# Top-k attention with a mixture of experts on one core: the scores of two heads copied out of PSUM together

## The chip, the cores and the metric

One core of one Trainium2 chip runs the program. The metric is device time in microseconds (us). The kernel before took 651.46 us (median of 3 runs, 651.18 to 654.83). The profile comes from one more execution of 652.79 us.

## The reference

Three parts follow each other. All the work of this case is in the first, the attention:

```python
B, H, S, D = 2, 8, 576, 64            # q, k, v
scores = q @ k.T / sqrt(D)            # per batch and head: 576 x 576
kth = 32nd largest of each row
attn = softmax(where(scores >= kth, scores, -1e9))
x = attn @ v                          # then 1152 tokens x 512
```

Then each token goes to one of 8 experts (`argmax` of 8 gate logits, at most 288 tokens for each), two matmuls with a ReLU between; then a dense layer 512 to 2048 to 512 with `h * clip(h + 3, 0, 6) / 6`. All is float32.

## The kernel before, in words

The attention is cut into 72 units: 9 tiles of 128 tokens by 8 heads. A unit u is one head of one tile, so its scores are 128 rows of 576 columns. Tile 4 holds 64 tokens of each batch; its units 32 to 39 take a query of all 128 rows (two heads, the other half zeros), and their last product is done in two halves.

Nothing is scheduled by the tool: the order is written out. A loop over steps i = 0 to 72 (L568) runs a string of letters, `STEP = "RGXCYTZEMAQLB"` (L36), and each letter issues one block for a unit that lies a fixed number of steps back or ahead (L557). Each engine takes its own instructions in that order, in a queue. The letters that matter here, with the engine, and the unit in step i:

| letter | what | engine, lines | unit |
|---|---|---|---|
| C | `cut_excess` | ScalarE (ACT), L337 | i - 1 |
| Y | `fetch`: scores from PSUM to SBUF | ACT, L313 | i + 2 |
| Z | `shift` | ACT, L396 | i - 3 |
| E | `expo`, out of PSUM | ACT, L421 | i - 4 |
| M | `below`, the mask of what is under the 32nd value | ACT, L400 | i - 3 |
| T | `ptr`: five transposes of Z's result, each with M's mask added by a matmul | TensorE (PE), L414, L415 | i - 4 |
| A | `attv`: five products with v | PE, L432 | i - 5 |
| Q | `qk`: scores of units i + 3 and i + 4, in odd steps alone | PE, L304 | i + 3, i + 4 |
| R, L | the search for the 32 largest | VectorE (DVE), L328 to L364 | |
| X, B | two subtractions of 128x576 | GpSimd (POOL), L334, L340 | |

On ACT a step is C, Y, Z, E, M; on PE it is T, A and in odd steps Q. T of a step reads what Z and M of the step before wrote, E reads what T of the same step wrote, A what E of the step before wrote. Q writes two PSUM tiles of two banks each (`ps_s`, L194); the copies Y of the next even step and of the odd step after it read them. Pairs of heads lie on rows 0 to 63 and 64 to 127, so the two products of a pair run beside each other on the array; in units 32 to 39 they take all rows and run one after the other.

Four times (steps 11, 15, 19, 23, and in each of steps 1 to 4) a block `mix` (L443) stands ahead of a step: ten PE records and two small ACT copies. In steps 43, 49, 55, 61 a scaled copy `xg` (L515, ACT) and an indirect DMA follow the step.

The experts begin after the attention, and then the dense layer; both are long runs of matmuls.

Of the kernel before, what the change touches and what calls it, by code (L numbers as in the profile page):

```python
# [8 lines left out]
F32 = mybir.dt.float32  # L9
F32R = mybir.dt.float32r  # L10
BF = mybir.dt.bfloat16
I32 = mybir.dt.int32
U32 = mybir.dt.uint32
AF = mybir.ActivationFunctionType
OP = mybir.AluOpType
AX = mybir.AxisListType
PS = bass.MemoryType.PSUM

P = 128
B, H, S, D = 2, 8, 576, 64  # L20
# [18 lines left out]
RING = 8  # L39
# [19 lines left out]
def topk_attention_moe_ffn_kernel(ctx, tc, qT, kT, vx, vT, wg, w1, w2, w_in, w_out, out, cap):  # L59
    nc = tc.nc  # L60
    W = 192
# [24 lines left out]
    rows = wp.tile([1, 2, E], F32, name="rows")  # L86
# [104 lines left out]
    with ExitStack() as actx:  # L191
        big = actx.enter_context(tc.tile_pool(name="big", bufs=1))
        wk = actx.enter_context(tc.tile_pool(name="wk", bufs=2))
        ps_s = actx.enter_context(tc.tile_pool(name="ps_s", bufs=2, space=PS))  # L194
        ps_t = actx.enter_context(tc.tile_pool(name="ps_t", bufs=1, space=PS))
        ps_o = actx.enter_context(tc.tile_pool(name="ps_o", bufs=2, space=PS))

# [10 lines left out]
        kt = big.tile([P, B, HP, S], F32, name="kt")  # L208
# [51 lines left out]
        for i in range(2):  # L260
            u = big.tile([P, 5 * P], F32, name=f"ub{i}")
# [18 lines left out]
        st, st2, tops, ends = {}, {}, {}, {}  # L280
        av, cuts = {}, {}
# [6 lines left out]
        def split(u):  # L288
            t, h = divmod(u, H)
            if t == 4:  # L290
                hp, b = h // 4 * 2 + h % 4 // 2, h % 2
                return [(b, 2 * hp + r, slice(b * 64, b * 64 + 64), slice(r * 64, r * 64 + 64)) for r in range(2)]
            return [(t // 5, h, slice(0, P), slice(0, P))]

        def qk(*us):
            todo = []
            for u in us:
                b, h = split(u)[0][:2]
                t, r0 = u // H, h % 2 * D
                rows, q = (slice(0, P), qts[b * 5 + 4]) if t == 4 else (slice(r0, r0 + D), qts[t])  # L300
                todo.append((u, ps_s.tile([P, 2, 512], F32, name="ps"), q[rows, h // 2], kt[rows, b, h // 2]))
            for c in range(2):
                for _, ps, q, k in todo:
                    nc.tensor.matmul(ps[:, c, :288], q, k[:, c * 288:(c + 1) * 288], start=True, stop=True)  # L304
            for u, ps, _, _ in todo:
                st[u] = ps

        def fetch(u):
            ps = st[u]
            slab = wk.tile([P, S * 3 // 2], F32, name="s", bufs=RING)  # L310
            cuts[u] = slab[:, S:].bitcast(BF)
            st[u] = slab[:, :S]
            nc.scalar.activation(st[u].rearrange("p (a b) -> p a b", a=2), ps[:, :, :288], AF.Copy)  # L313

        def interleave(*chains):
            chains = [list(c) for c in chains]
            n = max([1] + [len(c) for c in chains])
            for i in range(n):
                for ops in chains:
                    for f in ops[i * len(ops) // n:(i + 1) * len(ops) // n]:  # L320
                        f()
# [12 lines left out]
            nc.gpsimd.tensor_tensor(s2, s, lists[t % 2][:, h, KEEP * NCK:, None].to_broadcast([P, NCK, CW]), op=OP.subtract)  # L334

        def cut_excess(u):
            nc.scalar.activation(cuts[u], st2[u], AF.Relu, scale=PUSH)  # L337

        def drop_excess(u):
# [13 lines left out]
        def merge(u):  # L353
            t, h = divmod(u, H)
            l = lists[t % 2][:, h, NE - KT:KEEP * NCK]
            m = wk.tile([P, 2, KT], F32, name="m2")
            l2 = wk.tile([P, KEEP * NCK - NE + KT], F32, name="l2")
            end = ends.pop(u)
            for i in range(2):
                yield lambda i=i: nc.vector.max(m[:, i], l2 if i else l)  # L360
                yield lambda i=i: nc.vector.match_replace(out=l2, in_to_replace=m[:, i], in_values=l2 if i else l,
                                                          imm_value=LOW)
            yield lambda: nc.vector.max(end[:, NE:], l2)
            yield lambda: nc.vector.max(tops[t][:, h, KT:], end)  # L364
# [37 lines left out]
        def part(u):  # L402
            t, h = divmod(u, H)
            nc.vector.tensor_scalar(ubufs[u % 2][:, :S], st[u], -1.0, tops[t][:, h, 0:1], op0=OP.mult, op1=OP.add)

        def mask(u):
            t, h = divmod(u, H)
            nc.vector.tensor_scalar(lbufs[u % 2][:, :S], st.pop(u), tops[t][:, h, 2 * KT - 1:], None, op0=OP.is_lt)

        def ptr(u):  # L410
            pt = ps_t.tile([P, 8, P], F32, name="pt")
            for c in range(5):
                cs = slice(c * P, (c + 1) * P)
                nc.tensor.matmul(pt[:, c], ubufs[u % 2][:, cs], ident, is_transpose=True, start=True, stop=False)  # L414
                nc.tensor.matmul(pt[:, c], lbufs[u % 2][:, cs], drop, start=False, stop=True)  # L415
            st[u] = pt

        def expo(u):
            pt = st[u]
            pts = wk.tile([P, 5, P], F32, name="pts")  # L420
            nc.scalar.activation(pts, pt[:, :5], AF.Exp, scale=-SCALE)  # L421
            st[u] = pts

        def attv(u):
            t, g = u // H, u % H // 4
            pts = st.pop(u)
            if (t, g) not in av:
                av[t, g] = temp([P, 4, VC], "av")
            for b, h, rows, cols in split(u):
                for c in range(5):  # L430
                    at = (2 * c + h % 2) * VS
                    nc.tensor.matmul(av[t, g][rows, h % 4], pts[:, c, cols], vt[b, h // 2][:, at:at + VC],  # L432
                                     start=c == 0, stop=c == 4)

        def norm(t, h0, h1, rows=slice(0, P)):
            o = av.pop((t, h0 // 4))[rows, h0 % 4:h0 % 4 + h1 - h0]
            rs = wk.tile([P, 4, 1], F32, name="rs")[rows, :h1 - h0]
            yield lambda: nc.vector.tensor_scalar(rs, o[:, :, VS - 1:VS], 1e-9, None, op0=OP.add)
            yield lambda: nc.vector.reciprocal(rs, rs)
            yield lambda: nc.vector.tensor_tensor(x_tok[rows, t, h0:h1], o[:, :, :VS - 1],  # L440
                                                  rs.to_broadcast(list(o.shape[:2]) + [VS - 1]), op=OP.mult)
# [83 lines left out]
        def keep_warm(n, out):  # L525
            for _ in range(n):
                nc.tensor.matmul(out, dummy[:, :P], dummy, start=True, stop=True)
# [32 lines left out]
        keep_warm(KW, wm)  # L560
        load_q(2)
        qk(0, 1)
        fetch(0)
        fetch(1)
        qk(2, 3)
        for i in range(LEAD):
            interleave(round1(i))
        for i in range(NU + 1):  # L568
# [17 lines left out]
            for a, b, at, gap in ROUTES:  # L586
# [3 lines left out]
                n, r = divmod(i - at - 2, gap)  # L590
# [9 lines left out]
        u = NU - 1  # L600
        round2(u)
        interleave(merge(u - 1), merge(u), norm(NT - 1, 0, 4), routes[NU - 1][3])
        spare = ps_s.tile([P, 2, 512], F32, name="ps")[:, 0]
        warm = lambda n: keep_warm(n, spare)
        send = lambda t: scatter(t) if t >= sent else None
        for f, *args in ((ptr, u - 2), (expo, u - 2), (attv, u - 3), (send, 4), (send, 5), (attv, u - 2), (warm, 5),
# [10 lines left out]
        def redo(u):  # L617
            t, h = divmod(u, H)
            qk(u)
            fetch(u)  # L620
            s = st[u]
            tops[t] = wk.tile([P, H, 2 * KT], F32, name="tops")
            top = wk.tile([P, TOPK], F32, name="ends", bufs=4)
            m = top
            cur = s
            for i in range(4):
                nc.vector.max(m[:, 8 * i:8 * i + 8], cur)
                if i < 3:
                    nxt = wk.tile([P, S], F32, name="s2", bufs=3)
                    nc.vector.match_replace(out=nxt, in_to_replace=m[:, 8 * i:8 * i + 8], in_values=cur, imm_value=LOW)  # L630
                    cur = nxt
            nc.vector.tensor_copy(tops[t][:, h, 0:1], m[:, 0:1])
            nc.vector.tensor_copy(tops[t][:, h, 2 * KT - 1:], m[:, TOPK - 1:])
            part(u)
            mask(u)
            ptr(u)
            expo(u)
            last = (t, h // 4) in av
            attv(u)
            if last:  # L640
                return
            for n, (_, h, rows, _) in enumerate(split(u)):
                if n:
                    av[t, h // 4] = o
                o = av[t, h // 4]
                interleave(norm(t, h, h + 1, rows))
# [3 lines left out]
        with tc.If(at(0) > 0):  # L650
# [11 lines left out]
            for t in range(NT - 2):  # L662
# [2 lines left out]
            scale(NT - 2, xg_last[NT - 2])  # L665
            pick(NT - 2)
        room[0] = ps_o, "o"
        spare = ps_s.tile([P, 2, 512], F32, name="ps")[:, 0]

        t = NT - 1  # L670
        banks = [pool.tile([P, 2, 512], F32, name=name)[:, 0, :2 * W].rearrange("p (a w) -> p a w", a=2)
                 for pool, name in ((ps_s, "ps"), (ps_t, "pt"))]
        warm(WARM[0])
        interleave(norm(t, 4, H))
        x_pick(banks, xg_last[NT - 2], NT - 2, True)
# [11 lines left out]
    with ExitStack() as mctx:  # L687
# [59 lines left out]
        with ExitStack() as ectx:  # L747
            eb = ectx.enter_context(tc.tile_pool(name="eb", bufs=2))
            ps = ectx.enter_context(tc.tile_pool(name="ps", bufs=8, space=PS))
# [154 lines left out]
        ps = mctx.enter_context(tc.tile_pool(name="ps2", bufs=2, space=PS))  # L904
# [111 lines left out]
```

## Time and profile before

| | |
|---|---|
| median of the runs | 651.46 us |
| profiled execution | 652.79 us, span of the trace 651.0 us |
| PE busy | 614.4 us, 94% |
| ACT busy | 369.7 us, 57% |
| DVE busy | 370.6 us, 57% |
| POOL busy | 285.5 us, 44% |
| attention steps | from about 5 to 250 us of the span |
| copies of scores (L313) | 72, 48.4 us in all |

The shares are means over stages with different limits. In the attention ACT, PE and DVE are all at nine tenths or more; in the experts and the dense layer PE alone is. A busy time is the union of the spans of an engine's instructions. Two neighbours on ACT overlap by about a tenth of a us in the trace, so what an instruction takes of its engine is read from start to start, and when its result is there from its start and its duration.

### The profile page before, as it was taken

What the parts mean: (1) busy time and instruction counts of PE and PEld (TensorE: products, weight loads), DVE (VectorE), ACT (ScalarE), POOL (GpSimd) and SP (SyncE); (2) the same over time, 40 slices, a digit from 0 to 9 for tenths busy, and PEclk for the clock granted to TensorE, in tenths of its full rate; (3) what the DMA queues carried; (4) which work ended last, traced back from release to release, by engine and by line L of the source; (5) the groups of instructions that cost most, each with busy time, mean ns of one, the idle gap of its engine ahead of it and who ended that gap; (6) DMA issues with size and microseconds to landing.
All of it is one profiled execution on the core that took longest, in us unless ns stands there. A gap on an engine that the chain in (4) does not pass through costs nothing.

```text
span 651.0 us, 11922 instructions
## 1 busy us (share of the span) xinstructions
PE 614.4 (94%) x4085; PEld 549.7 (84%) x4085; DVE 370.6 (57%) x1838; ACT 369.7 (57%) x687; POOL 285.5 (44%) x337
## 2 busy tenths in 40 slices
PE   7899999999989987799999999999999999999996
PEld 4687878888767775699999999998988999999995
DVE  3899999999899994211233333334756655222221
ACT  3899999989999983111233343344555544242222
POOL 5787878869789962000234222222432342030001
PEclk9899999999999998899999999999999999999999
DMA  8529700100000002297789977712331320010001
GB/s 284 183 69 367 239 2 17 34 3 18 18 17 3 16 2 80 103 332 289 188 258 284 306 285 263 254 65 65 98 98 65 97 65 1 0 66 33 1 1 48
DMA packets 37054, 75.13 MB, mean 115 GB/s; under 512 B 4016, under 2 KB 12464, under 8 KB 36976
## 3 DMA queue, kind: packets, MB, share of 16 engines
q1 hardware_dynamic: 35248, 69.47, 32.4%
q0 software_dynamic: 1728, 4.72, 1.9%
q8 instruction: 36, 0.59, 0.4%
q14 instruction: 42, 0.34, 0.2%
HBM read 64.75 MB, written 9.44 MB: 114 GB/s over the span
## 4 chain that ended last, share of the span: by engine, by line
PE 42%; issue 14%; POOL 2%; ACT 0%; POOLq 0%; DVE 0%; ACTq 0%; DVEq 0%
PE hps L806 13%; PE yps L806 13%; PE h L915 8%; PE acc L929 7%; POOL out_dram L938 1%; PE xp L769 1%; POOL cm__12092 L723 0%; POOLq L1012 0%; POOL spacer L937 0%; ACT cg__11220 L715 0%; POOL fw L730 0%; ACT fw L729 0%; ACT gh L922 0%; DVE cg__11220 L717 0%; DVE x2l L826 0%
## 5 line engine op out<-in xcount | busy, mean ns | idle before, releaser
L328 DVE MAX8 lists<-s 128x8 f32<-128x72 f32 x576 | 127.5, 228 | 17.3 <-ACT s L313 17.1
L340 POOL TENSOR_TENSOR s<-s 128x576 f32<-128x576 f32 x72 | 92.5, 1285 | 34.2 <-ACT s L337 33.8
L915 PE MATMUL h<-x2h,fw 128*128 128x384 f32 x384 | 98.5, 337 | 0.9 <-DVE x2l L826 0.9
L432 PE MATMUL av<-vt,pts 128*128 128x96 f32 (+1 forms) x800 | 99.3, 273 | 0.0
L432 PEld LDWEIGHTS av<-vt,pts 128*128 128x128 f32 (+1 forms) x800 | 91.0, 182 | 2.1 <-issue 0.9
L806 PE MATMUL yps<-hT,wslot 128*128 128x192 f32 x512 | 90.8, 326 | 0.0
L806 PE MATMUL hps<-xe,wslot 128*128 128x192 f32 x512 | 86.4, 330 | 3.5 <-DVEq L844 2.9
L929 PE MATMUL acc<-fw,gh 128*128 128x512 f32 x288 | 89.4, 391 | 0.0
L806 PEld LDWEIGHTS hps<-xe,wslot 128*128 128x128 f32 x512 | 85.1, 193 | 4.1 <-ACT xg L858 3.4
L334 POOL TENSOR_TENSOR s<-s,lists 128x576 f32<-128x576 f32 x72 | 82.9, 1152 | 4.8 <-DVE lists L328 3.6
L806 PEld LDWEIGHTS yps<-hT,wslot 128*128 128x128 f32 x512 | 82.1, 190 | 1.2
L414 PE MATMUL pt<-ident,ub 128*128 128x128 f32 x360 | 76.2, 289 | 6.7 <-ACT pts L421 6.1
L415 PE MATMUL pt<-drop,lb 128*128 128x128 bf16 x360 | 66.2, 221 | 9.4 <-ACT lb L400 9.4
L915 PEld LDWEIGHTS h<-x2h,fw 128*128 128x128 f32 x384 | 70.2, 188 | 5.0 <-DVE x2l L826 1.2
L414 PEld LDWEIGHTS pt<-ident,ub 128*128 128x128 f32 x360 | 51.1, 142 | 25.5 <-ACT pts L421 9.9
L915 PE MATMUL h<-x2l,fw 128*128 128x384 f32 x192 | 64.8, 337 | 0.0
L929 PEld LDWEIGHTS acc<-fw,gh 128*128 128x128 f32 x288 | 53.4, 187 | 8.3
L918 ACT ACTIVATE g<-h,three 128x384 f32<-128x384 f32 x48 | 27.9, 581 | 56.2 <-PE h L915 56.2
L919 DVE SCALAR_TENSOR_TENSOR g<-g,h 128x384 f32<-128x384 f32 x48 | 26.5, 552 | 54.7 <-ACT g L918 54.2
L400 ACT ACTIVATE lb<-s,tops 128x576 bf16<-128x576 f32 x71 | 57.6, 811 | 0.0
L922 ACT CAST gh<-g 128x384 fp32r<-128x384 f32 x48 | 24.6, 513 | 56.8 <-PE acc L929 52.1
L396 ACT ACTIVATE ub<-s,tops 128x576 f32<-128x576 f32 x70 | 56.6, 809 | 0.0
(411 smaller groups left out, 1018.7 us busy)
## 6 DMA issues: line engine op xcount, KB each, us to landing
wslot<-in_w_dram SPq DMA_DIRECT2D x15, 2048.0 KB, 9.7
raw<-in_w_in_dram SPq DMA_DIRECT2D x16, 512.0 KB, 3.7
raw<-in_w_out_dram SPq DMA_DIRECT2D x16, 512.0 KB, 3.6
xs<-x_tok SPq DMA_DIRECT2D x8, 576.0 KB, 13.0
vt<-in_vx_dram SPq DMA_DIRECT2D x8, 365.0 KB, 4.6
kt<-in_kT_dram SPq DMA_DIRECT2D x8, 288.0 KB, 4.3
vts<-in_vT_dram SPq DMA_DIRECT2D x8, 288.0 KB, 4.1
qt<-in_qT_dram SPq DMA_DIRECT2D x9, 256.0 KB, 4.6
```

The source lines that it names most:

```text
L328: yield lambda c=c: nc.vector.max(lists[t % 2][:, h, c::NCK], st[u][:, c * CW:(c + 1) * CW])
L334: nc.gpsimd.tensor_tensor(s2, s, lists[t % 2][:, h, KEEP * NCK:, None].to_broadcast([P, NCK, CW]), op=OP.subtract)
L340: nc.gpsimd.tensor_tensor(st2[u], st[u], cuts.pop(u), op=OP.subtract)
L396: nc.scalar.activation(ubufs[u % 2][:, :S], st[u], AF.Identity, bias=tops[t][:, h, 0:1], scale=-1.0)
L400: nc.scalar.activation(lbufs[u % 2][:, :S], st.pop(u), AF.Relu, bias=tops[t][:, h, 2 * KT - 1:], scale=-1.0)
L414: nc.tensor.matmul(pt[:, c], ubufs[u % 2][:, cs], ident, is_transpose=True, start=True, stop=False)
L415: nc.tensor.matmul(pt[:, c], lbufs[u % 2][:, cs], drop, start=False, stop=True)
L432: nc.tensor.matmul(av[t, g][rows, h % 4], pts[:, c, cols], vt[b, h // 2][:, at:at + VC], start=c == 0, stop=c == 4)
L806: nc.tensor.matmul(out, wb[:, k], m[:, k, :self.w], start=first and k == 0, stop=last and k == HP - 1)
L915: nc.tensor.matmul(h2, fw[f][:, 0, a, k * P:(k + 1) * P], (x2h, x2l)[b][:, k, c * CH:(c + 1) * CH], start=n == 0, stop=n == len(ops) - 1)
L918: nc.scalar.activation(g, h2, AF.Relu, bias=three)
L929: nc.tensor.matmul(acc[j], g[a][:, j * P:(j + 1) * P], fw[f][:, 1, b], start=f == 0 and n == 0, stop=f == NF - 1 and n == 2)
```

## The change

The two score tiles of a pair become one PSUM tile of four banks with one buffer. Q writes its two halves with the same matmuls in the same order. `fetch` does nothing for odd units; for an even one, one ACT instruction copies both halves, 1152 columns, into one SBUF tile for two units. There are four such tiles where there were eight single ones. The result of C, which lay behind each unit's scores in the same buffer, gets a small tile of its own (three buffers). At the end of the attention two later users of that PSUM, the target of the idle matmuls (`spare`) and the first of `banks`, are two banks of one tile.

```diff
-        ps_s = actx.enter_context(tc.tile_pool(name="ps_s", bufs=2, space=PS))
+        ps_s = actx.enter_context(tc.tile_pool(name="ps_s", bufs=1, space=PS))
...
         def qk(*us):
             todo = []
+            room_s = ps_s.tile([P, 2, 2, 512], F32, name="ps")
+            st[us[0]] = room_s
             for u in us:
...
-                todo.append((u, ps_s.tile([P, 2, 512], F32, name="ps"), q[rows, h // 2], kt[rows, b, h // 2]))
+                todo.append((u, room_s[:, len(todo)], q[rows, h // 2], kt[rows, b, h // 2]))
...
-        def fetch(u):
+        def fetch(u, n=2):
+            if n == 2 and u % 2:
+                return
             ps = st[u]
-            slab = wk.tile([P, S * 3 // 2], F32, name="s", bufs=RING)
-            cuts[u] = slab[:, S:].bitcast(BF)
-            st[u] = slab[:, :S]
-            nc.scalar.activation(st[u].rearrange("p (a b) -> p a b", a=2), ps[:, :, :288], AF.Copy)
+            slab = wk.tile([P, 2, S], F32, name="s", bufs=RING // 2)
+            for i in range(n):
+                st[u + i] = slab[:, i]
+            nc.scalar.activation(slab[:, :n].rearrange("p u (a b) -> p u a b", a=2), ps[:, :n, :, :288], AF.Copy)
...
         def cut_excess(u):
+            cuts[u] = wk.tile([P, S], BF, name="cut", bufs=3)
             nc.scalar.activation(cuts[u], st2[u], AF.Relu, scale=PUSH)
...
         qk(0, 1)
         fetch(0)
-        fetch(1)
         qk(2, 3)
...
-        spare = ps_s.tile([P, 2, 512], F32, name="ps")[:, 0]
+        ends_ps = ps_s.tile([P, 2, 2, 512], F32, name="ps")
+        spare = ends_ps[:, 1, 0]
```

ACT, two steps from the first tile, an odd and then an even one, before (`s<-s` is C, `s<-ps` is Y, `ub` is Z, `pts` is E, `lb` is M):

```order
L337 ACTIVATE s<-s_571 128x576 [waits Pool_49]
L313 ACTIVATE s<-ps 128x576
L396 ACTIVATE ub_188<-s,tops 128x576 [waits Activation_49]
L421 ACTIVATE pts<-pt 128x640 [waits PE_49,Activation_49]
L400 ACTIVATE lb_190<-s,tops 128x576 [waits DVE_49,Activation_49]
L337 ACTIVATE s<-s_621 128x576 [waits Pool_49]
L313 ACTIVATE s<-ps 128x576 [waits PE_49]
L396 ACTIVATE ub_192<-s,tops 128x576 [waits Activation_49]
L421 ACTIVATE pts<-pt 128x640 [waits PE_49,Activation_49]
L400 ACTIVATE lb_194<-s,tops 128x576 [waits DVE_49,Activation_49]
```

The same two steps now:

```order
L340 ACTIVATE cut<-s_562 128x576 [waits Pool_49]
L399 ACTIVATE ub_188<-s,tops 128x576 [waits Activation_49]
L424 ACTIVATE pts<-pt 128x640 [waits PE_49,Activation_49]
L403 ACTIVATE lb_190<-s,tops 128x576 [waits DVE_49,Activation_49]
L340 ACTIVATE cut<-s_613 128x576 [waits Pool_49]
L315 ACTIVATE s<-ps 128x1152 [waits PE_49,Activation_49]
L399 ACTIVATE ub_192<-s,tops 128x576
L424 ACTIVATE pts<-pt 128x640 [waits PE_49]
L403 ACTIVATE lb_194<-s,tops 128x576 [waits DVE_49]
```

The odd step has lost its copy; the copy of the even step is twice as wide and still stands ahead of Z, E and M of its step, behind a wait for PE.

PE, the end of an odd step and the start of the next, before (`av` is A, `ps` is Q, `pt` is T):

```order
L432 MATMUL av<-vt_118,pts 128x96 x4
L304 MATMUL ps<-kt,qt 128x288
L304 MATMUL ps<-kt,qt 128x288 [waits Activation_49]
L304 MATMUL ps<-kt,qt 128x288 x2
L414 MATMUL pt<-ident,ub_188 128x128 [waits Activation_49]
L415 LDWEIGHTS lb_190 [waits Activation_49]
```

And now:

```order
L435 MATMUL av<-vt_118,pts 128x96 x4
L306 MATMUL ps<-kt,qt 128x288 x4
L417 MATMUL pt<-ident,ub_188 128x128 [waits Activation_49]
L418 LDWEIGHTS lb_190 [waits Activation_49]
```

Q no longer waits inside for the copy of the odd step; its place behind A and ahead of T is as it was. SP's queue is the same in both.

## Rows read from the trace of the kernel before

**Rows 1.** Busy us of PE, PEld, DVE, ACT, POOL in one stretch; granted clock, DMA.

```profile
90.00:130.00 40.00, 38.23 (x315) 32.86 (x315) 38.35 (x265) 39.52 (x65) 34.28 (x42) 1.00 0.07 21
```

**Rows 2.** ACT in order of time, one pair of steps: start us, duration us, line.

```profile
63.06 0.78 ACT L400 ACTIVATE lb<-s,tops 128x576 bf16<-128x576 f32 x1
63.72 0.69 ACT L337 ACTIVATE s<-s 128x576 bf16<-128x576 f32 x1
64.30 0.65 ACT L313 ACTIVATE s<-ps 128x576 f32<-128x576 f32 x1
...
66.75 0.69 ACT L337 ACTIVATE s<-s 128x576 bf16<-128x576 f32 x1
67.32 0.65 ACT L313 ACTIVATE s<-ps 128x576 f32<-128x576 f32 x1
67.85 0.79 ACT L396 ACTIVATE ub<-s,tops 128x576 f32<-128x576 f32 x1
68.52 0.71 ACT L421 ACTIVATE pts<-pt 128x640 f32<-128x640 f32 x1
69.10 0.79 ACT L400 ACTIVATE lb<-s,tops 128x576 bf16<-128x576 f32 x1
```

**Rows 3.** PE in order of time, the same pair; idle before and its releaser in brackets.

```profile
63.89 0.23 PE L415 MATMUL pt<-drop,lb 128*128 128x128 bf16 x1 [0.34 <-ACT lb L400]
...
64.64 1.31 PE L432 MATMUL av<-vt,pts 128*128 128x96 f32 x10
65.88 1.24 PE L304 MATMUL ps<-kt,qt 64*128 64x288 f32 x8
67.05 0.33 PE L414 MATMUL pt<-ident,ub 128*128 128x128 f32 x1
```

**Rows 4.** Waits of ACT from 30 to 234 us: us in total, times, longest.

```profile
ACT s L313 <- PE ps L304: 1.0, 2, 0.6
```

**Rows 5.** ACT, two of its lines: duration ns min/median/max, forms.

```profile
L313 ACT ACTIVATE s<-ps x72: 633/652/827, 6.3 to 231.2; 128x576 f32<-128x576 f32 x72
L816 ACT ACTIVATE hT<-hps x64: 314/331/332, 271.0 to 433.2; 128x192 f32<-128x192 f32 x64
```

**Rows 6.** PE in order of time, units of tile 4 in A.

```profile
130.27 1.24 PE L304 MATMUL ps<-kt,qt 64*128 64x288 f32 x8
...
134.41 0.22 PE L415 MATMUL pt<-drop,lb 128*128 128x128 bf16 x1
```

**Rows 7.** ACT, the same stretch.

```profile
131.54 0.65 ACT L313 ACTIVATE s<-ps 128x576 f32<-128x576 f32 x1 [0.37 <-PE ps L304]
...
133.34 0.77 ACT L400 ACTIVATE lb<-s,tops 128x576 bf16<-128x576 f32 x1
```

**Rows 8.** PE, units of tile 4 in Q.

```profile
110.32 2.13 PE L304 MATMUL ps<-kt,qt 128*128 128x288 f32 x8
```

**Rows 9.** ACT, M of the even steps around that Q.

```profile
107.60 0.76 ACT L400 ACTIVATE lb<-s,tops 128x576 bf16<-128x576 f32 x1
...
114.00 0.77 ACT L400 ACTIVATE lb<-s,tops 128x576 bf16<-128x576 f32 x1
```

**Rows 10.** PE at a step with `mix`.

```profile
69.10 1.37 PE L447 MATMUL mix<-wg_sb,vts 128*128 128x96 f32 x10
```

**Rows 11.** PE, Q in the first steps.

```profile
8.74 1.24 PE L304 MATMUL ps<-kt,qt 64*128 64x288 f32 x8 [2.51 <-DMA kt<-in_kT_dram]
...
12.84 1.23 PE L304 MATMUL ps<-kt,qt 64*128 64x288 f32 x6 [0.27 <-ACT s L313]
...
18.30 1.23 PE L304 MATMUL ps<-kt,qt 64*128 64x288 f32 x6 [0.62 <-ACT s L313]
```

**Rows 12.** Busy us by stretch as in group 1, in the clock's dip.

```profile
24.00:26.00 2.00, 1.70 (x11) 1.45 (x12) 1.84 (x14) 2.00 (x5) 1.36 (x2) 0.60 0.60 230
26.00:28.00 2.00, 2.00 (x12) 1.88 (x11) 2.00 (x16) 1.85 (x4) 1.36 (x3) 0.55 0.01 3
```

**Rows 13.** The chain that ended last, its first long piece after the attention.

```profile
269.40 11.91 PE hps L806 x62
```

More of the change, by code (lines that the diff above doesn't have):

```diff
@@ L304, in qk @@
                     nc.tensor.matmul(ps[:, c, :288], q, k[:, c * 288:(c + 1) * 288], start=True, stop=True)
-            for u, ps, _, _ in todo:
-                st[u] = ps
-        def fetch(u):
+        def fetch(u, n=2):
+            if n == 2 and u % 2:
+                return
             ps = st[u]
-            slab = wk.tile([P, S * 3 // 2], F32, name="s", bufs=RING)
-            cuts[u] = slab[:, S:].bitcast(BF)
-            st[u] = slab[:, :S]
-            nc.scalar.activation(st[u].rearrange("p (a b) -> p a b", a=2), ps[:, :, :288], AF.Copy)
+            slab = wk.tile([P, 2, S], F32, name="s", bufs=RING // 2)
+            for i in range(n):
+                st[u + i] = slab[:, i]
+            nc.scalar.activation(slab[:, :n].rearrange("p u (a b) -> p u a b", a=2), ps[:, :n, :, :288], AF.Copy)
         def interleave(*chains):
@@ L602, in topk_attention_moe_ffn_kernel @@
         interleave(merge(u - 1), merge(u), norm(NT - 1, 0, 4), routes[NU - 1][3])
-        spare = ps_s.tile([P, 2, 512], F32, name="ps")[:, 0]
+        spare = ps_s.tile([P, 2, 2, 512], F32, name="ps")[:, 0, 0]
         warm = lambda n: keep_warm(n, spare)
@@ L619, in redo @@
             qk(u)
-            fetch(u)
+            fetch(u, 1)
             s = st[u]
@@ L667, in topk_attention_moe_ffn_kernel @@
         room[0] = ps_o, "o"
-        spare = ps_s.tile([P, 2, 512], F32, name="ps")[:, 0]
+        ends_ps = ps_s.tile([P, 2, 2, 512], F32, name="ps")
+        spare = ends_ps[:, 1, 0]
         t = NT - 1
-        banks = [pool.tile([P, 2, 512], F32, name=name)[:, 0, :2 * W].rearrange("p (a w) -> p a w", a=2)
-                 for pool, name in ((ps_s, "ps"), (ps_t, "pt"))]
+        banks = [tile[:, :2 * W].rearrange("p (a w) -> p a w", a=2)
+                 for tile in (ends_ps[:, 0, 0], ps_t.tile([P, 2, 512], F32, name="pt")[:, 0])]
         warm(WARM[0])
```

## The prediction

> **What bounds the kernel now.** I read the busy time by stretch first. In a 40 us stretch of the attention ACT is busy 39.5 us, DVE 38.4, PE 38.2, POOL 34.3 [rows 1]. ACT is the fullest, but three others are near, so a share tells little: what matters is which wait returns to ACT. Then ACT and PE in order of time over one pair of steps. ACT runs without a gap: from M of one even step to M of the next it takes 69.10 - 63.06 = 6.04 us, a start every 0.53 to 0.67 us [rows 2]. PE waits 0.34 us for M's mask, then does the rest of T, then A, then Q [rows 3]. So a loop goes round both engines once a pair: M of the even step, T, A and Q of the odd step, copy Y, Z, E, M of the next even step. It is nearly as long as ACT's own work. M ends at 63.06 + 0.78 = 63.84; PE goes on at 63.89; Q starts at 65.88 and ends at 67.12 [rows 2, 3]; a copy that does wait for Q starts 0.03 us after its end (131.54 against 130.27 + 1.24) [rows 6, 7]. So the copy could have started at 67.15, and started at 67.32 [rows 2]: **the slack of the loop is 0.17 us.** That is why ACT waits for Q only twice, 1.0 us in all, between 30 and 234 us [rows 4]. What the attention loses or gains is passed on whole, since the experts' matmuls begin only after it [rows 13].
>
> **The change, part by part.**
>
> *ACT's own work.* 36 copies go and 36 grow. The copy takes 0.53 us from its start to Z's (67.32 to 67.85) [rows 2]. Per element, from the shortest copy of 576 and the shortest ACT instruction of 192 columns out of PSUM: (633 - 314) / 384 = 0.831 ns [rows 5], so 576 more columns cost 0.48 us. A pair saves 0.53 - 0.48 = 0.05 us, 1.8 us in all, if nothing but ACT counts. The Trainium skill (ScalarE: Activation LUTs, "What ACT_TABLE_LOAD costs") has neighbours overlap by about 93 ns, so each removed instruction would give that much, as an estimate 36 x 93 ns = 3.3 us; its 0.833 ns an element agrees with the trace's 0.831.
>
> *The loop.* All of the wide copy now stands between Q and M: 0.48 us more, where the loop had 0.17. From a row where the copy did wait, copy start to M's end is 133.34 + 0.77 - 131.54 = 2.57 us [rows 7]; the wide copy makes it 3.05. A plain pair is then: M's end to Q's end 67.12 - 63.84 = 3.28, plus 0.03, plus 3.05 = 6.36 us, against 6.04 to 6.05 now: **0.31 us more.** ACT then idles before the wide copy. The bounds of the second half are 0.48 (elements alone) and 0.53 (a whole further copy [rows 2]); I take 0.48, since it is one instruction.
>
> *The pairs*, by the odd step that holds Q; there are 34:
> - 11 plain ones (7, 25, 27, 45, 47, 53, 57, 59, 63, 65, 67): 11 x 0.31 = **3.4 us.**
> - Four with units of tile 4 in Q (29 to 35). The two heads run one after the other; Q takes 2.13 us, and the old copy needed only the first head. Now it waits for both. M ends at 107.60 + 0.76 = 108.36, Q at 110.32 + 2.13 = 112.45, so the next M ends at 112.45 + 0.03 + 3.05 = 115.53: 7.17 us, where M to M was 6.40 [rows 8, 9]. 4 x 0.77 = **3.1 us.**
> - Four with units of tile 4 in A (37 to 43). Here PE runs without a gap, and M's end (134.11) is 0.30 us ahead of the matmul that needs it (134.41) [rows 6, 7], 0.25 us with the 0.05 us that PE takes to start. The first such pair loses 0.48, the others about 0.24 each: **1.2 us.**
> - Eight with `mix` or just ahead of it (9 to 23): `mix` holds PE for 1.37 us between A and T [rows 10], so M may come 0.31 us later before T notices. **0**; the cover is PE's own work, and without it this would be another 2.5 us.
> - Four with the scaled copy for a scatter, or right behind one (49, 51, 55, 61): it fills the place that the odd copy leaves on ACT, so ACT and not Q is last there. **0.**
> - The first three (1 to 5). The first wide copy ends 0.48 us later, but the second Q waits for a transfer until 8.74 us anyway. After it Q waits twice for the copy of the odd step, 0.27 and 0.62 us [rows 11]; that copy is now done a step earlier, so both waits go: **-0.9 us.** Right behind lies a dip of TensorE's clock to 0.60 and 0.55 of full speed from 24 to 28 us [rows 12]; I leave it as it is. If the moved work escapes it, 2 x 0.40 + 2 x 0.45 = 1.7 us more is saved.
>
> *What else moves.* DVE may begin the search in a new pair only when the wide copy is done, 0.48 us later after its start, but has 38.35 of 40 us of work, 5.8 us in a pair of 6.05 [rows 1], so 0.56 us of room in 6.36. POOL has more. C's result in a tile of its own changes no transfer and no order. Q's PSUM is read out some 4 us before the next Q needs it, so one buffer costs PE nothing in the loop. The two PSUM users at the end keep their order on PE. All these: 0.
>
> **Sum**: 3.4 + 3.1 + 1.2 + 0 + 0 - 0.9 = 6.8 us. Against the profiled execution, 652.79, that is 659.6; it lay 1.3 us above the median, 651.46, which becomes **658.3 us.**
>
> **The rivals.**
> - *ACT alone is the bound* (not slower). If the loop had 0.48 us of slack or more, the change would give 0.05 us a pair: 651.5 - 1.8 = 649.7 us. It decides on one number, the time from Q's end to the copy's start in plain pairs. For it: ACT has no gaps [rows 2]. Against it: that time is 0.20 us, of which 0.03 is the wait itself. By the Trainium skill's 93 ns (ScalarE: Activation LUTs, the same section) it would be 648.2. Chance 0.08.
> - *Only the tight places pay.* If plain pairs have some slack that I don't see (a copy that starts reading sooner, a shorter T), what is left is 3.1 + 1.2 - 0.9 = 3.4 us: 654.9 us. For it: ACT hardly ever waits for Q now [rows 4]. Against: the starts fit to 0.05 us all along the pair. Chance 0.12.
> - *A further engine joins the loop.* If DVE, with its later start, holds M back, the pair grows by the rest of the 0.48 us too: 34 x 0.17 = 5.8 us more, 664 us. Or PE's longer gaps (in the four wide pairs over 1 us of 7.17) bring the clock down as at 24 us: each such dip costs 1.7 us, three of them 663 us. For it: DVE is 96% busy [rows 1]. Against: the clock stands at 1.00 through that stretch with PE not quite full, and DVE has the 0.56 us. Chance 0.12.
>
> **How the numbers follow.** The forecast has 0.68. Its own range: down by the clock's dip, 1.7, and some of the places called 0; up by 0.05 us in 19 pairs, 1.0, and 0.3 for the end of the attention: 656.0 to 659.5. The range reaches down to the second rival and up by half of the third: 654 to 662, which leaves out the first and most of the third, 0.2. A measurement of this kernel tells about 1% from no change, 6.5 us or 658.0. The forecast lies on that line: I give 0.38 of its 0.68 to slower by more, as the dip probably stays, 0.30 to within. With the rivals: slower 0.38 + 0.11 = 0.49; within 0.30 + 0.08 + 0.12 = 0.50, less 0.01 for the unforeseen; faster 0.02.
>
> **What would show it.** ACT should wait for Q (`s` of the copy behind `ps`) in nearly every pair between 30 and 234 us, about 0.4 us in a plain pair, where it now does twice. A plain pair should take 6.36 us from M to M, one with units of tile 4 in Q 7.17, one with `mix` what it takes now. The wide copy should last 1.12 us. The wait of 0.62 us in the first steps should be gone. It is wrong if ACT has no gap before the wide copy, if the gap is there and M to M still stays at 6.05, or if DVE or POOL is what M waits for.

## The result, and the profile after

The changed kernel takes 663.67 us in the median (four runs, 660.55 to 665.72). The kernel before stands at 653.14 over four runs, the three behind 651.46 and one more. The ratio is **1.0145, 95% interval 1.0108 to 1.0182: slower by about 9.5 us** (the medians lie 10.5 us apart). The forecast was 6.8 us more, and 658.3 us. The two profiled executions stand at 662.85 and 652.79 us.

The stretch of 40 us again, as in [rows 1]:

```profile
90.00:130.00 40.00, 35.47 (x277) 29.88 (x278) 34.59 (x241) 34.87 (x53) 31.93 (x41) 1.00 0.03 9
```

Every engine is busy for less of it: ACT 34.87 us instead of 39.52, PE 35.47 instead of 38.23. No engine became the bound; all of them wait more. ACT in order of time over one pair shows where (Q in step 9; like the pair of [rows 2] it lies just ahead of `mix`, and it takes what a plain pair takes):

```profile
37.51 0.77 ACT L403 ACTIVATE lb<-s,tops 128x576 bf16<-128x576 f32 x1
38.18 0.68 ACT L340 ACTIVATE cut<-s 128x576 bf16<-128x576 f32 x1
38.75 0.77 ACT L399 ACTIVATE ub<-s,tops 128x576 f32<-128x576 f32 x1
...
40.67 0.68 ACT L340 ACTIVATE cut<-s 128x576 bf16<-128x576 f32 x1
41.68 1.13 ACT L315 ACTIVATE s<-ps 128x1152 f32<-128x1152 f32 x1 [0.33 <-PE ps L306]
42.70 0.77 ACT L399 ACTIVATE ub<-s,tops 128x576 f32<-128x576 f32 x1
43.37 0.69 ACT L424 ACTIVATE pts<-pt 128x640 f32<-128x640 f32 x1
43.95 0.77 ACT L403 ACTIVATE lb<-s,tops 128x576 bf16<-128x576 f32 x1
```

And PE over the same pair:

```profile
38.34 0.23 PE L418 MATMUL pt<-drop,lb 128*128 128x128 bf16 x1 [0.34 <-ACT lb L403]
...
39.09 1.31 PE L435 MATMUL av<-vt,pts 128*128 128x96 f32 x10
40.33 1.24 PE L306 MATMUL ps<-kt,qt 64*128 64x288 f32 x8
```

These answer to [rows 2] and [rows 3]. M to M is 43.95 - 37.51 = 6.44 us, where it was 6.04. The loop is to be seen whole: M's end 38.28, PE goes on at 38.34, Q ends at 40.33 + 1.24 = 41.57. ACT has been waiting since cut ended, and starts the wide copy at 41.68. From M's end to Q's end it is 3.29 us, as before (3.28). What has grown is the copy (1.13 us), and the time from Q's end to its start, 0.11 us.

Waits of ACT, 30 to 234 us, as in [rows 4]:

```profile
ACT s L315 <- PE ps L306: 11.4, 21, 1.1
```

1.0 us in 2 waits have become 11.4 us in 21. They are the plain pairs, those just ahead of `mix` and those with units of tile 4, but for one. The copy's line by itself, with durations in ns (min, median, max), answers to [rows 5]:

```profile
L315 ACT ACTIVATE s<-ps x36: 1113/1131/1133, 7.5 to 237.2; 128x1152 f32<-128x1152 f32 x36
L315 ACTq EVENT_SEMAPHORE  x31: 17/17/17, 28.7 to 237.1; - x31
```

The second row is new: ahead of 31 of the 36 copies ACT's queue runs an instruction that only waits. The Trainium skill (Perfetto Trace Analysis, "Identifying Dependency Chains") says that an instruction with waits on several engines may get such a one ahead of it for the further wait; experiment 5 bears that out.

With units of tile 4 in Q, the rows that answer to [rows 8, 9]:

```profile
105.31 0.77 ACT L403 ACTIVATE lb<-s,tops 128x576 bf16<-128x576 f32 x1
...
107.78 1.13 ACT L315 ACTIVATE s<-ps 128x1152 f32<-128x1152 f32 x1 [1.12 <-PE ps L306]
...
112.54 0.77 ACT L403 ACTIVATE lb<-s,tops 128x576 bf16<-128x576 f32 x1
```

M to M is 7.23 us there, and ACT waits for 1.12 of them.

**The sum by place.** All pairs, from the end of M in one even step to the next, in the two profiles:

| pairs | forecast, us each | measured, us each | forecast, sum | measured, sum |
|---|---|---|---|---|
| 11 plain | 0.31 | 0.38 | 3.4 | 4.2 |
| 4 with units of tile 4 in Q | 0.77 | 0.83 | 3.1 | 3.3 |
| 4 with units of tile 4 in A | 0.48, 0.24 x 3 | 0.56, 0.33, 0.25, 0.42 | 1.2 | 1.6 |
| 4 just ahead of `mix` | 0 | 0.38 | 0 | 1.5 |
| 4 with `mix` | 0 | -0.29 | 0 | -1.1 |
| 4 at the scatters | 0 | -0.06 to -0.02 | 0 | -0.2 |
| from M of step 6 to M of step 68 | | | **7.7** | **9.2** |

A second profile of each kernel (experiments 8 and 12) gives this stretch as 199.15 us before (199.12 in the first) and 208.35 after (208.37). So the 9.2 us are of the kernel, to 0.03 us. What lies ahead of step 6 and between the attention and the experts is not so firm; it comes in the experiments.

### The profile page after: what moved, and what is told of

The parts are those of the page before. It is cut to its first block, busy times and chain, and to the rows that moved or that the text cites. A ratio compares the mean times of both kernels' runs of the same rounds, so it can differ in the third digit from the quotient of the medians.

```text
span 661.0 us, 11850 instructions
## 1 busy us (share of the span) xinstructions
PE 617.2 (93%) x4085; PEld 550.8 (83%) x4085; DVE 369.7 (56%) x1838; ACT 369.5 (56%) x651; POOL 286.1 (43%) x337
## 4 chain that ended last, share of the span: by engine, by line
PE 41%; issue 14%; POOL 2%; ACT 0%; POOLq 0%; DVE 0%; ACTq 0%; DVEq 0%
PE hps L809 13%; PE yps L809 12%; PE h L918 8%; PE acc L932 7%; POOL out_dram L941 1%; PE xp L772 1%; POOL cm__12055 L726 0%; POOLq L1015 0%; POOL spacer L940 0%; ACT cg__11183 L718 0%; POOL fw L733 0%; ACT fw L732 0%; ACT gh L925 0%; DVE cg__11183 L720 0%; DVE x2l L829 0%
## 5 line engine op out<-in xcount | busy, mean ns | idle before, releaser
L343 POOL TENSOR_TENSOR s<-s,cut 128x576 f32<-128x576 f32 x72 | 92.5, 1285 | 39.7 <-ACT cut L340 37.9
L932 PE MATMUL acc<-fw,gl 128*128 128x512 f32 x144 | 56.5, 392 | 0.0
L926 DVE TENSOR_TENSOR gl<-g,gh 128x384 fp32r<-128x384 f32 x48 | 27.4, 571 | 50.4 <-ACT gh L925 50.4
```

The costliest lines, as they stand in the source:

```text
L343: nc.gpsimd.tensor_tensor(st2[u], st[u], cuts.pop(u), op=OP.subtract)
L926: nc.vector.tensor_tensor(gl, g, gh.bitcast(F32), op=OP.subtract)
L932: nc.tensor.matmul(acc[j], g[a][:, j * P:(j + 1) * P], fw[f][:, 1, b], start=f == 0 and n == 0, stop=f == NF - 1 and n == 2)
```

## The experiments

My theory was that of the prediction: a loop through PE and ACT, M, T, A, Q, copy, Z, E, M, which the copy's width makes longer. The rivals were that DVE, which starts its search later, holds M back (the third rival of the prediction), and that the shared PSUM tile, not the width, costs the time. "M to M" is meant as above.

**1. q_ahead.** Q is put ahead of T and A, so that it no longer stands between M and the wide copy.

```
-STEP = "RGXCYTZEMAQLB"
+STEP = "RGXCYQTZEMALB"
```

> The changed kernel with one letter of the step's order moved: Q (the scores of the next pair, on PE) stands ahead of T and A of its odd step, not behind them. The wide copy stays as it is. My theory (the wide copy lies in a loop M, T, A, Q, copy, Z, E, M that goes round PE and ACT once a pair): Q then ends long before the copy's turn on ACT, the loop is cut, ACT is the bound again with the 0.05 us it saved a pair. M to M of a plain pair 6.0 to 6.1 us (changed kernel 6.44, before 6.06), with units of tile 4 in Q 6.1 to 6.3 (7.23); ACT hardly waits for Q; time 0.993 to 1.001 of before. Rival 1 (one instruction over four PSUM banks or one PSUM buffer costs by itself): M to M stays near 6.44, ratio near 1.0145. Rival 2 (DVE or POOL has joined the loop because a pair's scores come at once): M to M 6.2 to 6.4 and DVE or POOL named in front of M or C.

Measured: 651.06 us against 655.72 for the kernel before beside it, ratio **0.9927, interval 0.9899 to 0.9955**. ACT in a pair:

```profile
43.66 0.67 ACT L340 ACTIVATE cut<-s 128x576 bf16<-128x576 f32 x1
44.23 1.12 ACT L315 ACTIVATE s<-ps 128x1152 f32<-128x1152 f32 x1
45.24 0.77 ACT L399 ACTIVATE ub<-s,tops 128x576 f32<-128x576 f32 x1
```

No gap stands ahead of the wide copy any more. A plain pair takes 6.00 us instead of 6.44. With units of tile 4 in Q it takes 6.40, which is less than 7.23 but not the 6.1 to 6.3 expected. The first steps, by stretches as in [rows 12]:

```profile
22.00:24.00 2.00, 1.66 (x18) 1.59 (x18) 2.00 (x15) 2.00 (x4) 1.70 (x2) 1.00 0.92 355
24.00:26.00 2.00, 1.68 (x18) 1.43 (x17) 2.00 (x18) 2.00 (x4) 1.94 (x3) 1.00 0.10 38
26.00:28.00 2.00, 2.00 (x17) 1.44 (x15) 2.00 (x15) 2.00 (x4) 1.73 (x2) 1.00 0.00 0
```

The clock stays at 1.00 where it stood at 0.60 and 0.55. M of step 6 ends at 28.31 us, 3.5 earlier than in the first profile of before; from there to step 68 it is 198.25 us against 199.12. So the change with Q moved is faster than both kernels, and most of that gain lies in the first steps. The width costs nothing once it stands off the loop.

**2. copy_last.** Q stays where it is, and the copy goes to the end of ACT's step instead, behind M.

```
-STEP = "RGXCYTZEMAQLB"
+STEP = "RGXCTZEMYAQLB"
```

> The changed kernel with the copy Y moved behind M in its even step on ACT (order C, Z, E, M, Y); Q stays behind T and A. My theory: Z, E and M no longer stand behind the wait for Q, the loop is cut at another place, M to M of a plain pair 6.0 to 6.1 us; DVE gets the scores some 2 us later in the pair and may wait more, up to 6.2. Time 0.993 to 1.004 of before. Rival 1 (the wide instruction costs by itself): near 6.44 and 1.0145 as in the changed kernel. Rival 2 (DVE is what is short): slower than the changed kernel, above 1.015, with DVE's idle time in front of the search grown by over 0.4 us a pair.

Measured: 666.44 us, ratio 1.0154, interval 1.0113 to 1.0195. A miss for my theory. Plain pairs mostly alternate between 7.12 and 6.35 us. Waits from 30 to 245 us:

```profile
POOL s L336 <- DVE lists L347: 36.3, 34, 2.3
...
DVE lists L330 <- ACT s L315: 23.0, 30, 1.1
...
ACT lb L403 <- DVE tops L367: 11.0, 15, 1.1
```

Now ACT's M waits for DVE's tops, 15 times, since the search began late. So the rival with DVE is real, one move further on: the copy has a place that is too late for PE's loop and one that is too late for DVE's.

**3. two_copies.** Both heads in the even step, but in two instructions of 576 columns.

```
-nc.scalar.activation(slab[:, :n]..., ps[:, :n, :, :288], AF.Copy)
+for i in range(n):
+    nc.scalar.activation(slab[:, i]..., ps[:, i, :, :288], AF.Copy)
```

> The changed kernel, but the wide copy is split into two instructions of 576 columns, back to back in the same even step. My theory (what counts is how much copy time stands between Q and M, not that it is one instruction): M to M of a plain pair 6.44 + 0.05 = 6.49 us, time 1.015 to 1.019 of before; in the pairs with units of tile 4 in Q the first copy need not wait for the second head, so 6.9 instead of 7.23 there. Rival (the one wide instruction is the cost, by its four banks or its two waits): M to M falls to 6.05 to 6.2, ratio 1.000 to 1.006.

Measured: 663.46 us, ratio 1.0129, interval 1.0096 to 1.0163, a little under the 1.015 expected. A plain pair takes 6.50 us, as expected, against 6.44: joining two copies is worth 0.05 to 0.06 us, and moving the second one onto the loop costs several times that. From step 6 to step 68 it is 209.88 us, 1.5 more than with the wide copy. With units of tile 4 in Q it takes 7.29 (expected 6.9, a miss): the first copy still waits for both heads, although it reads only one.

**4. own_steps.** The other half of the change alone: one PSUM tile of four banks for the pair, but each head copied in its own step as before.

```
+if u % 2 and n == 2:
+    ps, slab = half.pop(u)
+    st[u] = slab[:, 1]
+    nc.scalar.activation(st[u]..., ps[:, 1, :, :288], AF.Copy)
...
+nc.scalar.activation(st[u]..., ps[:, 0, :, :288], AF.Copy)
```

> The changed kernel with the copy alone undone: one PSUM tile of four banks with one buffer, one SBUF tile for two heads and the small tile for C's result stay; each head is copied by its own instruction of 576 columns in its own step, as before. My theory (the copy's width in the loop is the whole cost in the loop): M to M of a plain pair is 6.05 to 6.12 us (before 6.06, changed 6.44; up to 0.06 more for the second wait of the copy where ACT really waits), with units of tile 4 in Q 6.4 to 6.9; time 0.998 to 1.004 of before. Rival (PSUM without a second buffer, or the new tiles, cost): M to M 6.2 or more, ratio 1.007 to 1.015.

Measured: 656.87 us, ratio 1.0058, interval 1.0026 to 1.0090, above the 1.004 expected. M of the even steps around one Q, on ACT:

```profile
37.00 0.80 ACT L406 ACTIVATE lb<-s,tops 128x576 bf16<-128x576 f32 x1
...
43.04 0.82 ACT L406 ACTIVATE lb<-s,tops 128x576 bf16<-128x576 f32 x1
```

A plain pair takes 6.05 us, the same as before. With units of tile 4 in Q it takes 6.75, against 6.40. From step 6 to step 68 it is 200.44 us, 1.3 above the kernel before, and 4 x 0.35 = 1.4 accounts for it. So the shared tile costs where the two heads run one after the other, and nothing in plain pairs; the rest, 9.2 - 1.3 = 7.9 us, is the joined copy. The ratio's interval, 1.7 to 5.9 us, lies above these 1.3 us; M of step 6 ends at 31.74 us, as in the first profile of before, and what the profile has behind the attention does not stand out of the scatter, so the rest of it stays open.

**5. five_slabs.** A fifth slab in SBUF for the scores.

```
-slab = wk.tile([P, 2, S], F32, name="s", bufs=RING // 2)
+slab = wk.tile([P, 2, S], F32, name="s", bufs=RING // 2 + 1)
```

> The changed kernel with five SBUF tiles for the copied pairs instead of four, so that the wide copy has one semaphore to wait for (PE) where it has two now (PE and ACT's own). In the changed kernel the copy starts 0.11 us after Q's end where I had counted 0.03. Theory (the second wait is an instruction of its own on ACT's queue and takes about 0.08 us each time ACT really waits there): the copy starts 0.03 us after Q, M to M of a plain pair 6.36 instead of 6.44, some 27 pairs x 0.08 = 2.2 us saved, ratio 1.011 to 1.012. Rival (the 0.11 us is the wait for PE's last matmul, whatever else is waited for): M to M stays 6.44, ratio 1.0145.

Measured: 662.45 us, ratio 1.0114, interval 1.0081 to 1.0148; a plain pair 6.38 us instead of 6.44. Q of one pair on PE:

```profile
39.58 1.24 PE L306 MATMUL ps<-kt,qt 64*128 64x288 f32 x8
```

The copy behind it on ACT:

```profile
40.86 1.13 ACT L315 ACTIVATE s<-ps 128x1152 f32<-128x1152 f32 x1 [0.27 <-PE ps L306]
```

The copy starts at 40.86, 0.04 us after Q's end at 39.58 + 1.24 = 40.82, where it was 0.11, and the copy's line has no waiting instruction any more. From step 6 to step 68 it is 207.00 us, 1.4 less. The second wait was for ACT's own last read of the slab, by M of the even step before, which was done 3.4 us ahead of the copy's start (38.28 against 41.68 us in the changed kernel). A wait that had long been met cost 0.07 us at each start on the loop.

**6. q_ahead_on_before.** The same move of Q in the kernel before.

```
-STEP = "RGXCYTZEMAQLB"
+STEP = "RGXCYQTZEMALB"
```

> The kernel before with Q ahead of T and A of its odd step, and nothing else. In the kernel before ACT is the bound in plain pairs and the loop has 0.17 us of room, so cutting the loop gives nothing there: M to M 6.05 us. It can gain where PE bounds (units of tile 4 in A, 0.5 us once) and in the first steps, where PE has a gap that Q now fills. Time 0.993 to 0.999 of before; against the changed kernel with the same order (0.9927, plain pair 6.00) it is slower by about 0.05 us in some 27 pairs, 1.4 us. Rival (all of the gain of that kernel is the order, the wide copy gives nothing): plain pair 6.00 and ratio 0.992 to 0.993.

Measured: 718.93 us, ratio 1.0996, interval 1.0952 to 1.1040: the largest miss of the study. PE at Q of one pair:

```profile
60.82 1.50 PE L304 MATMUL ps<-kt,qt 64*128 64x288 f32 x6 [1.40 <-ACT s L313]
```

ACT around it, with the copy of the odd step first:

```profile
60.12 0.65 ACT L313 ACTIVATE s<-ps 128x576 f32<-128x576 f32 x1
60.65 0.78 ACT L396 ACTIVATE ub<-s,tops 128x576 f32<-128x576 f32 x1
64.21 0.70 ACT L421 ACTIVATE pts<-pt 128x640 f32<-128x640 f32 x1 [2.78 <-PE pt L415]
```

Such waits from 30 to 260 us, in total, times and longest:

```profile
PE ps L304 <- ACT s L313: 33.5, 27, 2.0
```

Q needs the PSUM of both heads, and the second is read out only by the copy of the same odd step, which ends at 60.77. PE stands 1.40 us for it, T comes late, and ACT stands 2.78 us for T. I had not seen that the early reading of both heads frees PSUM a step sooner, and that this is what lets Q move.

**7. filled_gap.** The change, with eight idle matmuls on PE in step 5, where PE has a gap of 2.2 us and the clock falls behind it.

```
+if i == 5:
+    keep_warm(8, ps_o.tile([P, 512], F32, tag="o", name="wm2"))
```

> The changed kernel with eight idle matmuls of 512 columns put on PE ahead of T in step 5, into a PSUM bank that is free, where PE waits 2.2 us for ACT in the first steps. Right after that gap TensorE's clock stands at 0.50 for some 7 us in the changed kernel, where it was 0.55 to 0.60 for 4 us before. Theory (the longer gap brought the longer dip, and with it went the 0.9 us that I had counted as a gain): the dip is gone or shorter than 4 us, M of step 6 ends at 28 to 30 us (31.8 in both kernels), the pairs keep 6.44 us, ratio 1.008 to 1.011. Rival (the dip comes whatever PE does there): clock and M of step 6 as in the changed kernel, ratio 1.0145.

Measured: 661.26 us, ratio 1.0111, interval 1.0067 to 1.0154; from step 6 to step 68 208.34 us, as with the change. The clock in the first steps, with the busy times as above, is 1.00 throughout:

```profile
22.00:24.00 2.00, 1.18 (x11) 0.69 (x10) 2.00 (x16) 2.00 (x5) 1.36 (x2) 1.00 1.03 384
24.00:26.00 2.00, 2.00 (x20) 1.80 (x19) 2.00 (x15) 2.00 (x4) 1.99 (x2) 1.00 0.56 220
26.00:28.00 2.00, 2.00 (x21) 1.56 (x18) 2.00 (x15) 1.68 (x3) 1.73 (x2) 1.00 0.03 12
```

M of step 6 ends at 29.80 us, 2.0 earlier than in the first profile of the change (31.84) and 0.7 earlier than in the second (30.49, experiment 8).

**8. changed_again.** The changed kernel, unaltered, a second profile.

> The changed kernel once more, for a second profile: which of its times repeat. The pairs (6.44 and 7.23 us) should repeat to 0.02 us. The dip of the clock in the first steps (M of step 6 at 31.84 us) and the wait of TensorE between the last idle matmul and the experts' first (4.25 us after, 2.89 and 0.58 before) I do not know: if they are the change's, they repeat within 0.3 us; if they are chance, they scatter by 1 us or more.

Measured: 661.68 us. The dip of the clock in the first profile of the change, by stretches as above:

```profile
22.00:24.00 2.00, 1.26 (x10) 0.97 (x11) 2.00 (x19) 2.00 (x4) 1.49 (x2) 0.90 1.03 391
24.00:26.00 2.00, 2.00 (x11) 2.00 (x10) 2.00 (x15) 1.98 (x4) 2.00 (x2) 0.50 0.47 183
26.00:28.00 2.00, 2.00 (x10) 1.37 (x9) 1.61 (x10) 0.21 (x1) 1.69 (x3) 0.50 0.03 12
28.00:30.00 2.00, 2.00 (x13) 1.17 (x10) 0.09 (x1) 1.25 (x2) 0.84 (x1) 0.50 0.00 0
```

The same stretches in this second profile:

```profile
22.00:24.00 2.00, 1.66 (x11) 1.22 (x11) 2.00 (x18) 1.81 (x3) 1.70 (x2) 0.60 0.99 384
24.00:26.00 2.00, 2.00 (x12) 2.00 (x10) 2.00 (x16) 1.76 (x3) 1.65 (x2) 0.55 0.14 52
26.00:28.00 2.00, 2.00 (x18) 1.38 (x18) 1.17 (x7) 0.73 (x2) 1.75 (x2) 1.00 0.00 0
```

One kernel, two lengths of the dip: the lower of the clock's two levels, 1.2 GHz, holds for some 7 us in one execution and for 3 to 4 in the other. M of step 6 ends at 31.84 and 30.49 us.

**9. q_ahead_two_copies.** Experiments 1 and 3 together.

> Q ahead of T as in q_ahead, but the two heads are read out by two copies of 576 columns back to back in the even step: the width of the one instruction is gone, the order stays. If the gain of q_ahead comes from Q being off the loop, and the merge itself is worth the 0.05 us a pair worked out from before (start to start 0.53 us against 0.48 us for 576 columns), a plain pair takes 6.05 us where q_ahead took 6.00, and the time is 36 x 0.05 = 1.8 us above q_ahead's 0.993: ratio 0.994 to 0.998. Rival: the merge itself carries the gain, and the time goes back to that of before: 1.000 or above, a plain pair 6.1 us or more.

Measured: 651.38 us against 654.83, ratio 0.9936, interval 0.9905 to 0.9966. A plain pair takes 6.06 us, against 6.00 in q_ahead. ACT never waits for Q, so this is the price of the second instruction alone. By the Trainium skill (ScalarE: Activation LUTs, "What ACT_TABLE_LOAD costs") an instruction of this kind takes 186 ns beside its elements, and neighbours overlap by about 93 ns, so a second one would cost 93 ns, as an estimate. Here 0.05 to 0.06 us was measured, with the copy on the loop and off it. The gain of q_ahead is thus the order and the early reading; the joined instruction adds some 0.05 us a pair, too little for the ratios to tell apart. In this profile the clock was at its lower level for some 3 us from 10.7 us on, behind a gap of PE of 2.79 us, and M of step 6 ends at 30.32 us, against 28.31 in q_ahead.

**10. q_ahead_five_slabs.** Experiments 1 and 5 together.

> q_ahead with a fifth slab for the scores. With Q off the loop the wide copy starts without a wait, so the second thing that it waits for (ACT's own last read of the slab) should cost nothing: ratio 0.992 to 0.994, a plain pair 6.00 us, as q_ahead. Rival: the second wait costs the same 0.06 us wherever it stands, and 34 pairs give 2 us: 0.989 to 0.990, a plain pair 5.94 us.

Measured: 649.75 us, ratio 0.9925, interval 0.9900 to 0.9950; a plain pair 6.00 us, as expected. But it does not test the price of a second wait off the loop, as it was meant to: in q_ahead, with four slabs, the copy's line has no waiting instruction either, so the fifth slab had none to take away.

**11. y_first_on_before.** Experiment 6 with the copy ahead of C on ACT.

```
-STEP = "RGXCYTZEMAQLB"
+STEP = "RGXYCQTZEMALB"
```

> The kernel before with Q ahead of T, and the copy of the odd step put ahead of C on ACT. In q_ahead_on_before PE stood at Q for that copy (27 waits, 33.5 us), which stood behind C and so behind the search. If that was all, the waits at Q go, and the unmerged kernel gets what q_ahead got but for 0.05 us a pair: a plain pair 6.05 us, about 3 us less in the first steps, ratio 0.994 to 0.998. Rival: C, half a microsecond later on ACT, makes the search and POOL late: a plain pair 6.1 to 6.6 us, ratio 1.00 to 1.03, with waits of POOL for C or of ACT for M's tops.

Measured: 690.60 us, ratio 1.0543, interval 1.0517 to 1.0569: a miss. Waits from 30 to 260 us:

```profile
PE ps L304 <- ACT s L313: 21.4, 28, 1.4
```

PE still waits for that copy, 28 times, 21.4 us (33.5 in experiment 6). The copy has moved forward by one instruction on ACT, but it still stands behind M of the even step, so the loop is now M, copy, Q, T, E, and M again. Within these orders the unmerged kernel doesn't get Q ahead for free.

**12. before_again.** The kernel before, unaltered, a second profile.

> The kernel before, a second profile. Two things of the first are looked at. The gap on PE between the last idle matmul and the experts' first matmul: 2.89 us in the first profile of before, 3.94 to 4.34 us in all the kernels with the shared tile. If the gap belongs to the kernel it is 2.8 to 3.0 us again; if it scatters, up to 4.3. And the clock from 24 to 28 us: 0.60 and 0.55 again, M of step 6 done at 31.8 us within 0.3, or another length of the dip, 1 to 3 us away.

Measured: 656.10 us, with M of step 6 at 32.99 us where it was 31.76, after a longer dip. The rows from 24 us, where [rows 12] had 0.60 and 0.55:

```profile
24.00:26.00 2.00, 1.88 (x13) 1.72 (x14) 1.84 (x13) 2.00 (x5) 1.36 (x3) 0.61 0.48 186
26.00:28.00 2.00, 2.00 (x10) 1.83 (x11) 2.00 (x15) 1.66 (x3) 1.36 (x2) 0.50 0.01 2
28.00:30.00 2.00, 2.00 (x9) 0.95 (x8) 0.04 (x1) 0.12 (x1) 2.00 (x2) 0.50 0.00 0
```

PE's gap ahead of the experts in this profile:

```profile
270.71 0.98 PE L806 MATMUL hps<-xe,wslot 128*128 128x192 f32 x2 [2.91 <-DVEq L844]
```

The same place in the first profile of the change:

```profile
278.96 12.32 PE L809 MATMUL hps<-xe,wslot 128*128 128x192 f32 x64 [4.25 <-PEq L847]
```

The shorter gap belongs to the kernel before (2.89 and 2.91), the longer one to those with the shared tile (3.94 to 4.34). But the experts' second product starts 34.65 and 36.71 us after the last M in the two profiles of before, and 35.63 and 35.90 after it in those of the change, so the gap gives no difference there that stands out of the scatter. What makes PE leave the branch that stands there (L847) later stays open.

## Why the prediction was wrong

The direction and the mechanism were right, and most of the places; the sum was too small, and the time, 663.67 us, lay above the range of 654 to 662. The step that failed is a term of the loop's sum, the time from Q's end to the copy's start, with 0.03 us where 0.11 was measured.

- **The loop.** Shown. The bracket between "ACT alone" and "a loop with 0.17 us of slack" went to the loop: ACT waits for Q in 22 of the 31 pairs of the table, 0.33 us in a plain one, and taking Q off the loop (experiment 1) takes the whole loss away. The rival by which only the tight places pay is ruled out by the plain pairs' 6.44 us.
- **The term mis-sized: from Q's end to the copy's start.** I took 0.03 us from a copy with one wait [rows 6, 7]. The wide copy has two things to wait for, PE and a slab, and starts after 0.11 us. Experiment 5 removes the second: 0.06 us a pair, 1.4 us from step 6 to step 68. That is nearly all of the 9.2 - 7.7 = 1.5 us by which the loop was underrated. The plain pair without it, 6.38 us, is within 0.02 of the 6.36 worked out. The range allowed nothing for this term: upward it had 0.05 us a pair for the copy's width, which came out as taken (1.13 us), 0.3 us for the end of the attention, and half of a rival that did not come.
- **`mix`.** I gave the eight pairs 0, since `mix` would cover M's lateness. Pair by pair it was otherwise, and over two it nearly held: those ahead of `mix` lose 0.38 like plain ones, and those with it give back 0.29, because ACT then waits the less for `mix`. Before and after, at step 11:

```profile
44.48 0.28 ACT L452 COPY vt<-mix 128x64 f32<-128x64 f32 x2 [0.60 <-PE mix L447]
44.95 0.28 ACT L455 COPY vt<-mix 128x64 f32<-128x64 f32 x2 [0.23 <-PE mix L450]
```

  Two such pairs together take 13.11 us, against 13.01 before; without the second wait (experiment 5) they take 13.05. So the net of 0.4 us, set at 0, is for the greater part the same mis-sized term.
- **Units of tile 4.** 7.23 us against 7.17, for the same 0.06. Experiment 4 divides the 0.83 us of loss: 0.35 for waiting on both heads (the second wait, which that kernel has too, among them), the rest for the width.
- **The first steps, -0.9.** The step as put held by half. Of Q's two waits for ACT the first went: the Q at 12.00 us waits for a transfer alone, 0.46 us. The second did not: Q still waits 0.59 us at 16.58 us, now for the wide copy of the pair before. That Q does end earlier, 17.82 us against 18.30 + 1.23 = 19.53 [rows 11]. How much of it reaches step 6 hangs on the clock's dip: M ends at 31.84 and 30.49 us after the change, at 31.76 and 32.99 before. The two means differ by 1.2 us in favour of the change, but one kernel's own two profiles differ by as much. The forecast of -0.9 is neither shown nor refuted.
- **DVE, POOL and the end: 0.** In the loop this held; DVE waits for the copy (18 waits, 19.0 us from 30 to 234 us), and neither ACT nor PE waits for DVE. From the last M of step 68 to that of step 73 the change saves 0.3 us.
- **The base.** The forecast's 651.46 us was a median of three runs. With more runs the kernel before stood at 653.14 to 655.72. Added to 653.14, the forecast of 6.8 us gives 659.9, against 663.67: 1.7 us of the 5.4 by which the time was missed are of the base, and the ratio's interval, 7.1 to 11.9 us, lies wholly above 6.8. Of the other 3.7 the loop has 1.5 and the -0.9 that isn't shown another 0.9; the rest is not placed, and lies within the scatter outside the loop.

## What to carry to other kernels

Before two instructions are joined to save an issue, look for a loop through other engines that passes through them: there the joined one costs its whole added width (0.48 us here) but for the loop's slack (0.17), and the saving is a tenth of that (0.05). Joining them may pay in another way, since it empties a buffer earlier; then the producer can be moved forward, and that, not the instruction saved, gave most of the 0.7% here. Part of it came by way of the clock in the first steps, which idle matmuls kept up as well (experiment 7). An instruction that starts on such a loop should wait for one thing only; a spare buffer takes a second wait away, even one that is always met in time.

## What the runs showed of the hardware

- A second wait on ACT that was long met (3.4 us before) costs time at the start of an instruction that the first one holds back: 0.11 us from Q's end to the copy's start, against 0.04 without it, and 1.4 us over 62 steps.
- In the first steps the granted clock falls to its lower level behind a gap of PE, for 3 to 7 us, and the length differs between executions of one kernel. The gap in the change:

```profile
22.40 0.33 PE L417 MATMUL pt<-ident,ub 128*128 128x128 f32 x1 [2.21 <-ACT pts L424]
```

  In the kernel before it was 1.73 us, ahead of T at 23.64 us. With the gap filled by idle matmuls, or shortened by Q to some 1.0 us, the clock stayed at 1.00 there; so it did in copy_last, where the gap at that place was 1.20 us. The gap alone does not settle it: 2.51 us ahead of Q at 8.74 us in the kernel before had no dip behind it.
